# First quad's keys and queries by casting GpSimd transfers issued first, in place of float32 transfers and casts

## The chip, the cores and the metric

The kernel runs on one core of one Trainium2 chip. A time is the device time of one launch in microseconds (us); of several runs the median is given. "PE" is TensorE (the matrix engine), "DVE" VectorE, "ACT" ScalarE, "POOL" GpSimd, and "SP" SyncE. ACT, SP and POOL can each start transfers (DMAs); a transfer started from POOL may change the number type on its way (here float32 in memory to bf16 on the chip), one started from ACT or SP copies.

## The reference, cut to what matters

```
q_l, k_l, v_l: [8 batches, 8 heads, 512, 64]      q_g, k_g, v_g: [8, 8, 32, 64]      float32
out_g = softmax(q_g @ [k_g, k_l]^T / 8) @ [v_g, v_l]                 # 32 global rows see all 544 keys
s_ll  = q_l @ k_l^T / 8, kept where |i - j| <= 32, else -1e9          # 512 local rows see a band ...
out_l = softmax([q_l @ k_g^T / 8, s_ll]) @ [v_g, v_l]                 # ... and the 32 global keys
x = concat([out_g, out_l]) as [8*544 tokens, 512]
h = x @ w_in        # 512 x 2048
out = (h * sigmoid(1.702 h)) @ w_out                                  # 2048 x 512, float32 [4352, 512]
```

## The kernel before, in words

Attention and the two-layer network are one program. Heads are handled four at a time: a *quad* is four heads of one batch, so each batch has two quads (`u` = 0 and 1). Batch 0's quads are `a = Quad(0)` and `c = Quad(1)`; later batches use `Wide` quads. The program's order is written out by hand (`tc.manual_schedule()`): every engine runs its own instructions in the order of the text, and waits only for data.

For a quad, the keys `rk` and queries `rq` (bf16, 128 partitions = 4 heads x 32 rows) are turned by DVE's 32x32 transpose into `kT` (`Tk`, L311) and into the query tile `qt` (`Tq`, L315). `ext` (L325) copies the turned global queries `qgT` into rows of `qt` beside the local ones. `B` (L339) writes the band into the score banks as a product of an identity and a bias; `S` (L356) adds the scores, in two rounds of windows (`S(0)`, `S(1)`); `X` (L384, L387) is ACT's exponential out of the banks into `e`; `K`/`XK` (L375, L411) are the scores against the global keys; `U`, `ekU` (L438, L423) sum probabilities and values, `R` (L462 to L466) takes reciprocals, `XL` (L471) scales into `xL`, the network's input. `h_mm` (L615) and `o_mm` (L655) are the network's two products; they are started as soon as `xL` of a batch is there, and from then on PE always has network work beside the next quads.

How the start is loaded, before the change. SP's queue brings the global queries of the first two quads in float32 (`load_g32("q")`, 64 KB, L137), then the two halves of the first quad's queries in float32 (`q32`, L150), then the global keys (`load_g32("k")`). ACT's queue brings the two halves of its keys (`k32`, L149). The float32 halves lie in a tile `early`. When they land, ACT casts the first key half and both query halves (`cast_act`, L782), DVE casts the second key half (L791) and the global queries and keys (`cast_g32`, L140). POOL first sets constants: `warm0`, ones, `bd` (a block mask), the ones columns of the value tiles, the triangle `step` (`affine_select`, L169), and the mask of the later batches (`mask_rest`, L228 to L230); from 3.57 us on it starts casting transfers: queries and keys of the second quad (`load(0, (1,))`, L81 and L82), global values (`load_turned`, L122 and L123), and then, in `load_rest()`, the values of batch 0 (L249, four transfers), the first weight `w_in` in eight transfers (L259, with the six `make_mask` copies, L225, ahead of the last two), the second weight `w_out`, the inputs of batch 1, and so on. All of POOL's transfers stand in one queue, q0, and are served in order. While nothing has landed, PE multiplies zeros (`fill`, L183): 21 times at the start, and 8 times between `B` and the first `S`.

The order of the first stage, as written:

```python
    cast_act(rk, k32, 0); cast_act(rq, q32, 0); cast_act(rq, q32, 1); cast_g32("q", rqg)
    transpose_g(0, 2, "q"); a.ext((0, 1)); a.Tk(0, 8)
    nc.vector.tensor_copy(rk[:, 0, halves[1]], k32[:, halves[1]])
    a.Tk(8, 16); a.Tq(0, 8); a.Tq(8, 16); a.ext((2, 3)); cast_g32("k", rkg); transpose_g(0, 2, "k")
    load_rest(); a.B(0); a.B(1, split=True); fill(8, a.bk[1][3])
    a.S(0, added=True, part=0); a.S(0, added=True, part=1); a.X(0); a.S(1, ...); zero(2, ...); a.X(1)
    c.Tq(); c.ext(); c.Tk(); c.B(0); a.K(); a.XK(); c.B(1, ...); c.S(0, added=True); c.X(0)
```

`S(0)` is split in two parts: part 0 needs the first half of the queries, part 1 also the second half.

Of the kernel before, what the change touches and what calls it, by code (L numbers as in the profile page):

```python
# [20 lines left out]
def kernel(  # L21
# [110 lines left out]
    def load_g32(name, src):  # L132
        t = g32[name] = consts.tile([128, 2, D], F32, name="g32%s" % name)
        if name == "v":
            load_turned(nc.sync, t, src[:, 0:2, :])
        else:
            nc.sync.dma_start(out=t, in_=src[:, 0:2, :])  # L137

    def cast_g32(name, t):
        nc.vector.tensor_copy(t[:, 0:2, :D], g32[name])  # L140

    load(0, kq=False)
    rk, rq = loaded[0]
    early = ld.tile([128, 4, TB], F32, name="early", bufs=1)
    k32, q32 = (early[:, 2 * i : 2 * i + 2].rearrange("p a b -> p (a b)") for i in range(2))
    halves = (slice(0, 8 * D), slice(8 * D, 16 * D))
    load_g32("q", qgf)
    for f in halves:
        nc.scalar.dma_start(out=k32[:, f], in_=kf[0][:, 0, f])  # L149
        nc.sync.dma_start(out=q32[:, f], in_=qf[0][:, 0, f])  # L150
    load_g32("k", kgf)


    warm0 = consts.tile([128, 128], BF16)
    nc.gpsimd.memset(warm0, 0.0)
    step = consts.tile([128, 289], BF16)
    nc.vector.memset(step, 1.0)
    ones32 = consts.tile([128, 32], BF16)
    nc.gpsimd.memset(ones32, 1.0)
    nc.gpsimd.memset(rvg[:, :, D:], 1.0)  # L160
    bd = consts.tile([128, 4, 32], BF16)
# [4 lines left out]
    for i in range(2):  # L166
        vtiles.append(consts.tile([128, 8 * 5 * (D + 2)], BF16, name="v%d" % i))
        nc.gpsimd.memset(v_view(i, 4 + i)[:, :, :, :, D:], 1.0)
    nc.gpsimd.affine_select(  # L169
        out=step, in_=step, pattern=[[1, 289]], compare_op=ALU.is_ge,  # L170
        fill=0.0, base=-97, channel_multiplier=-1,
    )
    w_in_sb = wts.tile([128, 4, NKC, d_ff // 4], BF16)
# [4 lines left out]
    warm = consts.tile([128, 512], BF16)  # L178
    nc.vector.memset(warm, 0.0)

# [5 lines left out]

    qtiles = []
    for i in range(4):
        qt = consts.tile([128, 24, 32], F32, name="q%d" % i)
        nc.vector.memset(qt[:, 0:4, :], 0.0)  # L190
        nc.vector.memset(qt[:, 20:24, :], 0.0)
        qtiles.append(qt)

# [37 lines left out]

    mask_rest()
    load(0, (1,))
    load_turned(nc.gpsimd, rvg[:, 0:2, :D], vgf[:, 0:2])

    qgT = consts.tile([128, NQ, 40], F32)
    nc.vector.memset(qgT[:, :, 32:], 0.0)
    kgT = consts.tile([128, NQ, 32], F32)
    def transpose_g(lo, hi, names="qk"):
# [49 lines left out]
    class Quad:  # L289
# [31 lines left out]

        def ext(self, cs=(0, 1, 2, 3)):
            for c in cs:
                (r0, nr), t0, n = WIN[c], (0, 20, 1, 20)[c], (4, 3, 3, 4)[c]
                nc.vector.tensor_copy(  # L325
                    self.qt[:, t0 : t0 + n, r0 : r0 + nr],
                    qgT[:, self.Q, : n * nr].rearrange("p (t r) -> p t r", t=n))
# [293 lines left out]

    spot = consts.tile([128, 2], F32)
    nc.gpsimd.memset(spot, 0.0)

    spot_p = consts.tile([1, 2], BF16)
# [154 lines left out]

    def cast_act(r, f32, hf):
        nc.scalar.activation(r[:, 0, halves[hf]], f32[:, halves[hf]], AF.Copy)  # L782
# [23 lines left out]
    zero(2, a.bk[1][3])  # L806
    a.X(1)
    c.Tq()
    c.ext()
    c.Tk()  # L810
    c.B(0)
# [42 lines left out]
    gelu(gTs[0][:, 2:4, :], pt[1])  # L854
    c.G()
    for fc in range(4, FC):
        h_step(0, fc)
# [337 lines left out]
```

## Time and profile before

| | us |
|---|---|
| median of 3 runs (288.1 to 288.44) | 288.11 |
| the profiled execution | 287.94 |
| its span, first to last instruction | 286.0 |
| PE busy | 280.4 (98%) |
| DVE busy / ACT busy / POOL busy | 205.3 / 184.5 / 95.3 |
| share of the 16 DMA engines' span: q0 (POOL's transfers) / q1 (SP's) / q10 (ACT's) | 55.9% / 11.5% / 0.7% |

Times in the text are counted from the start of the span. A row of the timeline reads: start, duration, engine, line of the program, operation, tile written <- tiles read, how many, and in brackets how long the engine stood idle before it and what ended that. In the list of transfers the last number is the median time from issue to landing. "q" behind an engine's name marks its sequencer, which issues transfers.

### The profile page before, as it was taken

What the parts mean: (1) busy time and instruction counts of PE and PEld (TensorE: products, weight loads), DVE (VectorE), ACT (ScalarE), POOL (GpSimd) and SP (SyncE); (2) the same over time, 40 slices, a digit from 0 to 9 for tenths busy, and PEclk for the clock granted to TensorE, in tenths of its full rate; (3) what the DMA queues carried; (4) which work ended last, traced back from release to release, by engine and by line L of the source; (5) the groups of instructions that cost most, each with busy time, mean ns of one, the idle gap of its engine ahead of it and who ended that gap; (6) DMA issues with size and microseconds to landing.
All of it is one profiled execution on the core that took longest, in us unless ns stands there. A gap on an engine that the chain in (4) does not pass through costs nothing.

```text
span 286.0 us, 8845 instructions
## 1 busy us (share of the span) xinstructions
PE 280.4 (98%) x3727; PEld 179.5 (63%) x3727; DVE 205.3 (72%) x494; ACT 184.5 (65%) x297; POOL 95.3 (33%) x142
## 2 busy tenths in 40 slices
PE   8999999999999999999999999999999999999995
PEld 7544445544554488646884488647874589448884
DVE  7771367787689898679867998679867697363452
ACT  4847657568678784778649774877658761874331
POOL 8984550855946003920086004800040000000001
PEclk9999999999999999999999999999999999999999
DMA  7999995999999801993059803940122003200213
GB/s 203 156 191 207 203 165 79 147 224 130 155 175 187 151 3 48 94 191 60 10 88 150 147 2 77 100 66 5 28 51 73 2 3 76 73 0 2 73 35 115
DMA packets 59351, 28.23 MB, mean 99 GB/s; under 512 B 47472, under 2 KB 49776, under 8 KB 59312
## 3 DMA queue, kind: packets, MB, share of 16 engines
q0 software_dynamic: 51760, 17.83, 55.9%
q1 hardware_dynamic: 7120, 9.18, 11.5%
q8 instruction: 29, 0.48, 0.7%
q10 hardware_dynamic: 432, 0.66, 0.7%
q14 instruction: 10, 0.08, 0.1%
HBM read 36.31 MB, written 8.91 MB: 158 GB/s over the span
## 4 chain that ended last, share of the span: by engine, by line
PE 93%; DVE 2%; ACT 2%; DMA 1%; issue 0%; SPq 0%; DVEq 0%
PE hp L615 38%; PE px L726 13%; PE py L726 9%; PE op L655 9%; PE x L726 6%; PE s L560 6%; PE ov L586 5%; PE s L615 2%; DMA early<-in_q_l_dram 1%; DVE xL L471 1%; ACT e L384 1%; PE og L597 1%; PE s L356 1%; PE s L339 1%; ACT e L387 1%; DVE rs L466 1%
## 5 line engine op out<-in xcount | busy, mean ns | idle before, releaser
L615 PE MATMUL hp<-xL,w_in_sb 128*128 128x512 bf16 x480 | 105.4, 379 | 0.1
L615 PEld LDWEIGHTS <-w_in_sb 128*128 128x128 bf16 x576 | 56.1, 98 | 60.0 <-issue 0.4
L620 ACT ACTIVATE gT<-hp 128x512 bf16<-128x512 f32 x120 | 69.8, 597 | 23.9 <-PE hp L615 22.4
L571 ACT ACTIVATE e<-s 128x1016 bf16<-128x1016 f32 (+1 forms) x56 | 53.3, 1002 | 20.3 <-PE s L560 20.2
L726 PEld LDWEIGHTS <-gs 128*128 128x128 bf16 x480 | 46.2, 98 | 6.7
L699 DVE TENSOR_TENSOR gs<-gT 128x512 bf16<-128x512 bf16 (+1 forms) x90 | 30.3, 364 | 17.7 <-ACT gT L620 17.2
L576 POOL TENSOR_TENSOR e<-e,mask 128x1760 bf16<-128x1760 bf16 x4 | 13.3, 3320 | 81.1 <-ACT e L571 81.1
L98 POOL DMA_DIRECT2D v<-in_v_l_dram x40 | 31.0, 777 | 14.9 <-PE og L597 3.9
L726 PE MATMUL py<-wsum,gs 128*128 128x256 bf16 x240 | 30.3, 273 | 0.0
L655 PE MATMUL op<-w_out_sb,gT 128*128 128x512 bf16 x128 | 29.5, 380 | 0.0
L576 DVE TENSOR_TENSOR e<-e,mask 128x1712 bf16<-128x1712 bf16 (+1 forms) x24 | 25.2, 1049 | 5.6 <-ACT e L571 5.6
L512 DVE STREAM_TRANSPOSE kT<-rk 128x512 f32<-128x512 f32 x14 | 14.6, 1045 | 14.9 <-DMA rk<-in_k_l_dram 14.9
L759 POOL DMA_DIRECT2D out_dram<-ob x2 | 1.2, 598 | 69.7 <-ACT ob L113 69.5
L655 PEld LDWEIGHTS <-gT 128*128 128x128 bf16 x128 | 11.8, 98 | 13.9
L726 PEld LDWEIGHTS <-gT 128*128 128x128 bf16 x192 | 18.0, 98 | 2.7
L726 PE MATMUL px<-w_out_sb,gT 128*128 128x256 bf16 x160 | 19.2, 273 | 0.0
L726 PE MATMUL px<-w_out_sb,gs 128*128 128x256 bf16 x160 | 19.1, 273 | 0.0
L471 DVE TENSOR_TENSOR xL<-ov,rs 128x512 bf16<-128x512 f32 x27 | 17.8, 685 | 0.7 <-PE ov L438 0.2
L696 DVE TENSOR_TENSOR gs<-gT 128x1024 bf16<-128x1024 bf16 (+1 forms) x30 | 17.4, 579 | 0.0
L560 PEld LDWEIGHTS <-kT 32*128 32x128 bf16 x672 | 12.6, 93 | 7.6 <-issue 6.7
L113 ACT ACTIVATE ob<-px 128x512 f32<-128x512 f32 x10 | 6.0, 598 | 15.2 <-DVE zz L748 15.2
L560 PE MATMUL s<-q,kT 32*128 32x160 bf16 (+1 forms) x448 | 14.9, 246 | 0.0
(150 smaller groups left out, 360.3 us busy)
## 6 DMA issues: line engine op xcount, KB each, us to landing
out_dram<-ob SPq DMA_DIRECT2D x128, 64.0 KB, 3.0
rq<-in_q_l_dram POOLq DMA_DIRECT2D x5, 512.0 KB, 8.0
rk<-in_k_l_dram POOLq DMA_DIRECT2D x5, 512.0 KB, 10.0
v<-in_v_l_dram POOLq DMA_DIRECT2D x24, 96.0 KB, 4.9
w_in_sb<-in_moe_w_in_dram POOLq DMA_DIRECT2D x8, 256.0 KB, 8.3
w_out_sb<-in_moe_w_out_dram POOLq DMA_DIRECT2D x4, 512.0 KB, 10.3
rq<-in_q_l_dram POOLq DMA_DIRECT2D x5, 256.0 KB, 8.5
rk<-in_k_l_dram POOLq DMA_DIRECT2D x5, 256.0 KB, 7.9
```

The lines of the kernel that those rows point to most:

```text
L98: nc.gpsimd.dma_start(out=vt[0:n, hs, c, :D], in_=vs[FIRST[c] : FIRST[c] + n, hs])
L471: nc.vector.tensor_mul(self.x[:, 2 * self.u + h, :], self.st[1 + h], self.st["rs"])
L512: nc.vector.transpose(flat[:, 0:Sl].rearrange("p (r t) -> p t r", t=16), loaded[self.b][0][:, self.u].bitcast(F32))
L560: nc.tensor.matmul(bank(self.ps, j)[:, at : at + n], lhsT=self.k[p, KEYS[c] : KEYS[c] + 128, e], rhs=qs[p, :, :, e], start=(e == 0), stop= ...
L571: nc.scalar.activation(self.E[rnd][:, 2 * i : 2 * i + 2, :n], self.ps[i][:, :, :n], AF.Exp, scale=scale)
L576: eng.tensor_mul(e, e, mask[:, rnd : rnd + 1, :n].to_broadcast([128, 4, n]))
L615: nc.tensor.matmul(hp[:, : width(i)], lhsT=w_in_c[:, fc // 4, kc, fc % 4 // 2, :, fc % 2], rhs=(xL[i] if i < B else xG)[:, kc, :], start=( ...
L620: nc.scalar.activation(out_, in_, AF.Gelu_apprx_sigmoid)
L655: nc.tensor.matmul(op, lhsT=gTs[i][:, fc, tci * 128 : tci * 128 + 128], rhs=w_out_sb[:, fc, :], start=(first and fc == 4 * f4), stop=(fc = ...
L696: nc.vector.tensor_tensor(sums[i][2][:, g, :n], t[:, g, 0, :n], t[:, g, 1, :n], ALU.add)
L699: nc.vector.tensor_tensor(sums[i][k][:, g, : n // 2], x[:, g], y[:, g], op)
L726: nc.tensor.matmul(out_, lhsT=lv[:, g, tt * 128 : tt * 128 + 128], rhs=rv[:, g, :], start=(g == 0 and k in ((1, 3, 4, 6) if self.apart els ...
```

## The change

Local keys and queries of the first quad are no longer brought as float32 by the queues of ACT and SP and then cast; POOL's casting transfers bring them straight into `rk` and `rq`, in four halves. They are POOL's first instructions: both key halves, then the triangle (`affine_select`), then both query halves, then the global keys of two quads (`load_g(0, 2, "k")`), then the second quad's keys and queries (keys first; before, queries first), and only then POOL's other constants and the global values. The global queries still come as float32 by SP's queue; their cast, and the first two copies of `ext`, go from DVE to ACT. An `exp_table()` call stands ahead of them on ACT. `warm0` and `spot` are set by DVE instead of POOL; DVE clears the query tiles of quads 0 and 1 only, and those of 2 and 3 after `c.G()`; the zero tile `warm` is set after the global keys' transpose. `mask_rest` moves from ahead of POOL's transfers into `load_rest`, ahead of the `make_mask` copies. `fill(8)` becomes `fill(2)`. For the second quad, `Tk` and `ext` now come ahead of `Tq`.

```diff
     def load_g32(name, src):
         t = g32[name] = consts.tile([128, 2, D], F32, name="g32%s" % name)
-        if name == "v":
-            load_turned(nc.sync, t, src[:, 0:2, :])
-        else:
-            nc.sync.dma_start(out=t, in_=src[:, 0:2, :])
-
-    def cast_g32(name, t):
-        nc.vector.tensor_copy(t[:, 0:2, :D], g32[name])
+        nc.sync.dma_start(out=t, in_=src[:, 0:2, :])
...
     load_g32("q", qgf)
     for f in halves:
-        nc.scalar.dma_start(out=k32[:, f], in_=kf[0][:, 0, f])
-        nc.sync.dma_start(out=q32[:, f], in_=qf[0][:, 0, f])
-    load_g32("k", kgf)
+        nc.gpsimd.dma_start(out=rk[:, 0, f], in_=kf[0][:, 0, f])
     warm0 = consts.tile([128, 128], BF16)
-    nc.gpsimd.memset(warm0, 0.0)
+    nc.vector.memset(warm0, 0.0)
     step = consts.tile([128, 289], BF16)
     nc.vector.memset(step, 1.0)
+    spot = consts.tile([128, 2], F32)
+    nc.vector.memset(spot, 0.0)
+    nc.gpsimd.affine_select(out=step, ...)
+    for f in halves:
+        nc.gpsimd.dma_start(out=rq[:, 0, f], in_=qf[0][:, 0, f])
+    load_g(0, 2, "k")
+    nc.gpsimd.dma_start(out=rk[:, 1], in_=kf[0][:, 1])
+    nc.gpsimd.dma_start(out=rq[:, 1], in_=qf[0][:, 1])
     ones32 = consts.tile([128, 32], BF16)
     nc.gpsimd.memset(ones32, 1.0)
     nc.gpsimd.memset(rvg[:, :, D:], 1.0)
+    load_turned(nc.gpsimd, rvg[:, 0:2, :D], vgf[:, 0:2])
+    (value tiles' ones columns, then bd)
...
-    nc.vector.memset(warm, 0.0)
-    for i in range(4): (clear qtiles[i])
+    clear_q(0, 1)
...
-    mask_rest()
-    load(0, (1,))
-    load_turned(nc.gpsimd, rvg[:, 0:2, :D], vgf[:, 0:2])
...
             if part == 3:
+                mask_rest()
                 for m in MASKS:
                     make_mask(m)
...
-    cast_act(rk, k32, 0)
-    cast_act(rq, q32, 0)
-    cast_act(rq, q32, 1)
-    cast_g32("q", rqg)
+    exp_table()
+    on_act(rqg[:, 0:2, :D], g32["q"])
     transpose_g(0, 2, "q")
-    a.ext((0, 1))
+    a.ext((0, 1), on_act)
     a.Tk(0, 8)
-    nc.vector.tensor_copy(rk[:, 0, halves[1]], k32[:, halves[1]])
     a.Tk(8, 16)
     a.Tq(0, 8)
     a.Tq(8, 16)
     a.ext((2, 3))
-    cast_g32("k", rkg)
     transpose_g(0, 2, "k")
+    nc.vector.memset(warm, 0.0)
     load_rest()
     a.B(0)
     a.B(1, split=True)
-    fill(8, a.bk[1][3])
+    fill(2, a.bk[1][3])
...
     a.X(1)
+    c.Tk()
+    c.ext()
     c.Tq()
-    c.ext()
-    c.Tk()
     c.B(0)
...
     c.G()
+    clear_q(2, 3)
```

More of the change, by code (lines that the diff above doesn't have):

```diff
@@ L144 @@
     early = ld.tile([128, 4, TB], F32, name="early", bufs=1)
-    k32, q32 = (early[:, 2 * i : 2 * i + 2].rearrange("p a b -> p (a b)") for i in range(2))
     halves = (slice(0, 8 * D), slice(8 * D, 16 * D))
@@ L148 @@
     for f in halves:
-        nc.scalar.dma_start(out=k32[:, f], in_=kf[0][:, 0, f])
-        nc.sync.dma_start(out=q32[:, f], in_=qf[0][:, 0, f])
-    load_g32("k", kgf)
+        nc.gpsimd.dma_start(out=rk[:, 0, f], in_=kf[0][:, 0, f])
     warm0 = consts.tile([128, 128], BF16)
-    nc.gpsimd.memset(warm0, 0.0)
+    nc.vector.memset(warm0, 0.0)
     step = consts.tile([128, 289], BF16)
     nc.vector.memset(step, 1.0)
+    spot = consts.tile([128, 2], F32)
+    nc.vector.memset(spot, 0.0)
+    nc.gpsimd.affine_select(
+        out=step, in_=step, pattern=[[1, 289]], compare_op=ALU.is_ge,
+        fill=0.0, base=-97, channel_multiplier=-1,
+    )
+    for f in halves:
[3 more added lines that the diff above has]
+    nc.gpsimd.dma_start(out=rq[:, 1], in_=qf[0][:, 1])
     ones32 = consts.tile([128, 32], BF16)
@@ L160 @@
     nc.gpsimd.memset(rvg[:, :, D:], 1.0)
+    load_turned(nc.gpsimd, rvg[:, 0:2, :D], vgf[:, 0:2])
+    for i in range(2):
+        vtiles.append(consts.tile([128, 8 * 5 * (D + 2)], BF16, name="v%d" % i))
+        nc.gpsimd.memset(v_view(i, 4 + i)[:, :, :, :, D:], 1.0)
     bd = consts.tile([128, 4, 32], BF16)
@@ L165 @@
         nc.gpsimd.memset(bd[32 * r : 32 * r + 32, j, :], 1.0)
[L166 to L172, printed above, removed]
     w_in_sb = wts.tile([128, 4, NKC, d_ff // 4], BF16)
@@ L185, with clear_q @@
     fill(21, psP.tile([128, 512], F32, name="w", tag="p"), True)
[L187 to L192, printed above, removed]
+    qtiles = [consts.tile([128, 24, 32], F32, name="q%d" % i) for i in range(4)]
+    def clear_q(*quads):
+        for i in quads:
+            nc.vector.memset(qtiles[i][:, 0:4, :], 0.0)
+            nc.vector.memset(qtiles[i][:, 20:24, :], 0.0)
+    clear_q(0, 1)
+    qgT = consts.tile([128, NQ, 40], F32)
+    nc.vector.memset(qgT[:, :, 32:], 0.0)
+    kgT = consts.tile([128, NQ, 32], F32)
     WIN = ((0, 10), (6, 12), (14, 12), (22, 10))
@@ L230, in mask_rest @@
         nc.gpsimd.memset(mask_at(1, 236, 16, 12)[96:128, :, 8:12], 0.0)
-    mask_rest()
-    load(0, (1,))
-    load_turned(nc.gpsimd, rvg[:, 0:2, :D], vgf[:, 0:2])
-    qgT = consts.tile([128, NQ, 40], F32)
-    nc.vector.memset(qgT[:, :, 32:], 0.0)
-    kgT = consts.tile([128, NQ, 32], F32)
     def transpose_g(lo, hi, names="qk"):
@@ L320, in T, with ext @@
             self.Tq()
-        def ext(self, cs=(0, 1, 2, 3)):
+        def ext(self, cs=(0, 1, 2, 3), copy=nc.vector.tensor_copy):
             for c in cs:
                 (r0, nr), t0, n = WIN[c], (0, 20, 1, 20)[c], (4, 3, 3, 4)[c]
-                nc.vector.tensor_copy(
+                copy(
                     self.qt[:, t0 : t0 + n, r0 : r0 + nr],
@@ L620, in gelu @@
         nc.scalar.activation(out_, in_, AF.Gelu_apprx_sigmoid)
-    spot = consts.tile([128, 2], F32)
-    nc.gpsimd.memset(spot, 0.0)
     spot_p = consts.tile([1, 2], BF16)
@@ L779, in zero @@
             nc.tensor.matmul(ps, lhsT=warm[:, 0:128], rhs=warm, start=False, stop=False, skip_group_check=True)
-    def cast_act(r, f32, hf):
-        nc.scalar.activation(r[:, 0, halves[hf]], f32[:, halves[hf]], AF.Copy)
-    cast_act(rk, k32, 0)
-    cast_act(rq, q32, 0)
-    cast_act(rq, q32, 1)
-    cast_g32("q", rqg)
+    exp_table()
+    on_act(rqg[:, 0:2, :D], g32["q"])
     transpose_g(0, 2, "q")
-    a.ext((0, 1))
+    a.ext((0, 1), on_act)
     a.Tk(0, 8)
-    nc.vector.tensor_copy(rk[:, 0, halves[1]], k32[:, halves[1]])
     a.Tk(8, 16)
```

## The prediction

> **What bounds the kernel now.** I read the page's busy times first, then the chain that ended last over the first 18 us (start, length, what), then the timelines of the engines, then the transfers' times to landing.
>
> ```profile
> PE 280.4 (98%) x3727; PEld 179.5 (63%) x3727; DVE 205.3 (72%) x494; ACT 184.5 (65%) x297; POOL 95.3 (33%) x142
> ```
> PE is busy nearly throughout, so only what PE waits for, or does in vain, can be saved. Its 5.6 us of idle time and its zero products lie mostly in the first 18 us; this change touches nothing later except through its transfers.
>
> ```profile
> 0.81 0.46 SPq L137
> 1.28 0.06 issue
> 1.34 4.16 DMA early<-in_q_l_dram
> 5.50 0.02 issue
> 5.52 1.27 ACT rq L782 x2
> 6.79 0.02 issue
> 6.81 0.46 DVE q L315
> 7.27 0.04 issue
> 7.31 0.47 PE s L356 x16
> 7.78 1.65 ACT e L387 x2
> 9.43 0.04 issue
> 9.47 0.63 PE s L339 x6
> ```
> The reader sees the start hang on one thing: the first quad's queries land at 5.50, ACT casts two halves, DVE turns the second one, and part 1 of the first scores starts at 7.31. From there on PE and ACT hand over to each other without idle time up to 17.8 us, where the network's products begin. What is saved ahead of 7.31 is saved at the end, unless another wait takes its place.
>
> ```profile
> 10.01 1.05 DVE L311 STREAM_TRANSPOSE kT<-rk 128x512 f32<-128x512 f32 x1 [0.48 <-DMA rk<-in_k_l_dram]
> 11.12 0.66 PE L356 MATMUL s<-q,kT 32*128 32x200 bf16 x16
> 32.85 1.04 DVE L512 STREAM_TRANSPOSE kT<-rk 128x512 f32<-128x512 f32 x1 [10.20 <-DMA rk<-in_k_l_dram]
> 37.30 0.53 PE L560 MATMUL s<-q,kT 32*128 32x160 bf16 x16
> ```
> Two such waits stand close behind. The second quad's keys land just before 10.01, and its scores start at 11.12, 0.06 us after the turned keys: no slack. Batch 1's keys land at 32.83, at the end of the stream of weights; DVE's and ACT's preparation for its scores ends at 36.02, and PE comes to them at 37.30: 1.27 us of slack.
>
> **The change part by part.** The sum is made in the profiled execution (287.94: span 286.0 and 1.94 around it; the median is 0.17 above it).
>
> *Casts taken away.* ACT's three (0.63 each) and DVE's second key half (0.40) and global keys (0.61) go. Of these 1.27 us lie on the chain, between 5.52 and 6.79; the others lie beside it.
>
> *When POOL issues.* POOL's, ACT's and SP's first instructions start at 0.81. An issue costs 0.71 for POOL's first (L81) and 0.56 for the next (L82); the triangle takes 0.37 from its start to the next start. So key halves at 0.81 and 1.52, triangle at 2.08 (DVE set `step` by 1.25 before; one small clear more ahead of it), query halves at 2.45 and 3.01, global keys at 3.57 (0.71, as L128), second quad's keys at 4.28 and queries at 4.84, done at 5.40.
>
> *When they land.* No row has a 128 KB casting transfer first in the program. Bounds: from below ACT's 128 KB of packets took 2.88 us from issue; from above a 256 KB casting one took 4.32 from an idle queue, less 0.65 for half of it (w_in's 256 KB pieces land 1.3 us apart in the full stream) makes 3.67. I take 3.24, which a 96 KB casting one took at 115.5 us, the nearest in size, kind and idle queue:
>
> ```profile
> rq<-in_q_l_dram POOLq DMA_DIRECT2D x1, 256.0 KB, 4.3
> v<-in_v_l_dram POOLq DMA_DIRECT2D x1, 96.0 KB, 3.2
> ```
> Key halves then land at 4.05 and, 0.65 later, 4.70; the first query half at 2.45 + 3.24 = 5.69 (the keys ahead of it would allow 5.35), the second at 6.34. With the ends for 3.24, the second lands at 5.99 or 6.77.
>
> *What follows.* DVE turns keys at 4.05 to 4.70 and 4.70 to 5.32 (0.60, 0.62), queries at 5.69 to 6.14 and 6.34 to 6.79 (0.45 each), against 7.26 before: 0.47 us. ACT's cast of the global queries waits for 3.86 at the latest and takes about 0.3 (ACT's 128x128 copy at 35.5: 0.26); the transpose is done by 4.5, and two copies on ACT (0.26 each) by 5.0: hidden behind the query half at 5.69. Uncovered they would cost 0.5. PE does 16 band products to 5.80 and 2 fills to 6.05; six fills fewer, 0.64 us, cost nothing before and would have ended at 6.65, so taking them away is needed but is no gain of its own.
>
> *Second quad.* Behind the second query half come 32 KB of global keys (rvg's 24 KB landed 0.25 behind the keys: 6.6), then 256 KB twice. These landed 1.73 apart before, and 1.25 in the full stream (half of w_out's 2.5); with 1.5, keys at 8.1 and queries at 9.6. DVE: keys to 9.15, ext (0.60) to 9.75, queries (0.71) to 10.46. PE comes at 11.12 - 0.47 = 10.65: 0.19 of slack; with 1.73 it would be 10.5 landing, 10.9 to 11.2 turned, and the gain is gone. Keys first is worth the 0.34 between the two turns, behind the last landing.
>
> *The stream behind.* POOL comes to batch 0's values later: 5.40, two small sets, global values 0.81 and 0.55, value tiles' and bd's sets 0.29 and 0.80: 8.0 against 6.24. But before, the first value transfer landed 0.45 behind the global values, so the engines that move the data were the limit, not POOL. Their work is the same bytes (2.3 us saved at q1 and q10 come back in q0) begun some 0.5 later. I take 0.4 for the stream's delay; bounds 0 and 1.76. Deadlines, with 0.47 off PE's times: fourth value transfer landed 15.01, needed by c.U(1) at 16.65; fourth w_in 20.00, needed at 21.66; batch 1's keys as above. They leave 1.2, 1.2 and 0.8: 0.4 fits. mask_rest (1.06) ahead of the masks puts w_in's last two issues at about 19.0 instead of 16.09; the sixth landed at 22.33, so the engines still have work for 3 us: nothing. POOL also waits, before an issue, for the transfer eight before it (20.29 followed a landing at 20.00, 21.34 one at 21.05); in the new order these landings are long past.
>
> *The rest.* clear_q(2, 3), four times 0.17, moves to about 22 us, where DVE is idle until 32.8; `warm` (0.27) goes behind the keys' transpose near 7.2, ahead of zero products at 8.4. Nothing.
>
> Sum: -0.47, rounded to -0.45: 287.49 for the profiled execution, **287.66** for the median.
>
> **A rule against the change.** DVE's cast of the global keys took 0.61 at 7.33 while POOL issued, and 0.23 for the same form at 3.88 with POOL issuing too: a collision of 0.38, once in two. The Trainium skill, SBUF — State Buffer, section "SBUF: two separate sides", says that a DVE copy in a two-port mode locks GpSimd out of writing descriptors, and advises the hardware queues instead. By that rule what goes on POOL here could start late by as much as DVE's eligible operations beside it; the trace shows the collision from DVE's side only.
>
> **The rivals.**
> (1) *Landing as by the hardware queue.* With 2.88 the second query half lands at 5.99, gain 0.82; PE then stops at the second quad's queries or at batch 1's keys (1.27 - 0.4), about -0.75: 287.36. For it: POOL's data packets start some 0.8 behind the end of an issue. Against: no load of POOL's landed in under 2.7, and that one had 48 KB.
> (2) *Second quad takes the place of the first.* Its queries land at 10.4, as its keys did at 9.99 before with the hardware queues helping: gain 0 to 0.1: 288.1. The 1.73 speaks for it, 1.25 against.
> (3) *The weights' stream moves by POOL's delay* (slower). If it shifts by 1.76, batch 1's keys land at 34.6, its preparation ends at 37.8, PE stands 0.5 after 37.30: 288.6; each 0.1 more that POOL takes adds 0.1. It decides from a shift of 1.27, and is a loss of 0.2% from 1.85. Against it: 0.45 between the landings named above.
> (4) *VectorE holds POOL's issues* (slower). Identity, band and bias on DVE (2.60 to 3.45) follow the triangle, exactly where the queries are issued. If all 0.85, and the small clears ahead of them (0.3), are lost, the second query half lands at 7.5, turned at 7.95: 0.7 later, 288.8. It decides from a hold of 0.47. For it: the collision above. Against: POOL's issue at 4.27 took 0.56 beside DVE copies.
> (5) *PE stays slow.* Fills came 0.107 us apart up to 6.65, band products 0.16; after 9.47 six of these took 0.63. If PE, idle from 6.05 for a late query, keeps its slow pace to about 10, 1.7 us of products ahead of 11.12 take some 1.1 more: 288.8. The profile's granted clock is 1.00 throughout and can't tell. The Trainium skill, TensorE: Matmul & The Clock Gate, section "What's actually happening", has a gate that doubles the rate after a busy window of about 3.4 us; the fills' pace agrees, its threshold no run here shows.
>
> **How the numbers follow.** Forecast 0.42 (gain 0.1 to 0.8; some 0.19 of it beyond 0.2%), rival 1 0.22, rival 2 0.08, rival 3 0.14, rival 4 0.09, rival 5 0.05. A difference of 0.2%, 0.58 us, is about what a measurement can tell from none. Faster: 0.19 + 0.21 = 0.40. Slower: most of rivals 3 to 5, 0.25. Within: 0.35. The range goes from rival 1 with a little more, 287.2, to rivals 3 to 5 at 288.8, leaving out about 0.16. The forecast's own is 287.3 to 288.0.
>
> **What would show it.** Query half 2 landed at 6.0 to 6.8 and turned by 7.2; first scores' part 1 at about 6.85; second quad's queries turned by 10.5 and its scores at 10.65; first w_in product near 17.4 instead of 17.8; batch 1's keys at 33.2, with no PE gap ahead of its scores. Wrong if POOL's issues take over 0.8 in the first 5 us, if a query lands past 6.8, if the scores' products stay 0.1 apart after 7, or if PE stands near 16, 21 or 37 us.

## The result, and the profile after

| | before | after |
|---|---|---|
| median, us | 288.11 (288.1 to 288.44) | **290.89** (290.4 to 293.05) |
| ratio to before | | 1.0104, 95% interval 1.0078 to 1.0131 |
| profiled execution / its span | 287.94 / 286.0 | 293.05 / 291.0 |
| first quad: last key half / last query half landed | 4.95 / 6.12 (float32) | 5.35 / 7.79 (bf16) |
| first exponentials (`X(0)`) start | 7.76 | 8.77 |
| second quad's last transfer landed | 9.99 | 13.30 |
| second quad's scores start on PE | 11.12 | 14.09 |
| first network product starts | 17.82 | 21.68 |
| batch 1's keys landed / its scores start | 32.83 / 37.30 | 38.84 / 42.05 |

The change costs 2.8 us, 1.0% (by the interval 2.2 to 3.8 us); the forecast was 287.66, range 287.2 to 288.8. The profiled execution of after is the longest of its four; the other three took 290.4, 290.4 and 291.38, so its times show where the loss arises and overstate how large it is at the median.

Busy times and granted clock in the page of after:

```profile
PE 281.1 (97%) x3721; PEld 179.4 (62%) x3721; DVE 203.5 (70%) x491; ACT 183.6 (63%) x298; POOL 97.8 (34%) x145
PEclk9979999999999999999999999999999999999999
```

PE's busy time hardly moved (280.4 before), so the loss is idle time, and work at a lower clock: the third slice (14.6 to 21.8 us) has a granted clock of 0.7 of full speed, where before every slice had the full one.

The chain that ended last, in after (start, length, what):

```profile
0.71 0.63 issue
1.34 1.25 POOL rk L142 x2
...
3.14 1.02 POOL rq L155 x2
...
8.30 0.78 POOL v L244
9.08 8.43 DMA v<-in_v_l_dram
...
17.79 0.71 POOL w_in_sb L255
...
19.68 2.30 POOL mask L227 x6
...
25.26 13.58 DMA rk<-in_k_l_dram
...
38.86 1.05 DVE kT L508
...
42.05 0.65 PE s L556 x24
```

Before, the chain left the transfers at 5.50 and then ran through ACT and PE. Here it runs through POOL and its queue for 39 us: first POOL's issues one behind the other, then the values, for which POOL waits before its sixth weight transfer, then the masks, then batch 1's keys.

The start of after on the engines (start, length, engine, line; in brackets the idle time before and what ended it):

```profile
1.34 1.25 POOL L142 DMA_DIRECT2D rk<-in_k_l_dram  x2 [0.82 <-POOLq L1167]
...
3.04 1.12 POOL L155 DMA_DIRECT2D rq<-in_q_l_dram  x2
...
4.81 0.60 POOL L157 DMA_DIRECT2D rk<-in_k_l_dram  x1
...
7.82 0.45 DVE L311 STREAM_TRANSPOSE q<-rq 128x256 f32<-128x256 f32 x1 [0.50 <-DMA rq<-in_q_l_dram]
8.32 0.92 PE L352 MATMUL s<-q,kT 32*128 32x80 bf16 x32 [0.43 <-DVE q L311]
11.62 1.04 DVE L307 STREAM_TRANSPOSE kT<-rk 128x512 f32<-128x512 f32 x1 [2.76 <-DMA rk<-in_k_l_dram]
11.88 0.71 POOL L255 DMA_DIRECT2D w_in_sb<-in_moe_w_in_dram  x1 [0.34 <-DMA rk<-in_k_l_dram]
13.32 0.71 DVE L311 STREAM_TRANSPOSE q<-rq 128x512 f32<-128x512 f32 x1 [0.41 <-DMA rq<-in_q_l_dram]
13.58 2.10 POOL L255 DMA_DIRECT2D w_in_sb<-in_moe_w_in_dram  x3 [0.99 <-DMA rq<-in_q_l_dram]
14.09 0.72 PE L352 MATMUL s<-q,kT 32*128 32x200 bf16 x16 [1.94 <-DVE q L311]
16.76 0.70 POOL L255 DMA_DIRECT2D w_in_sb<-in_moe_w_in_dram  x1 [1.07 <-DMA v<-in_v_l_dram]
```

Three things are to be read here. POOL's first transfer starts at 1.34, not 0.81, and the second query half can be turned only at 7.82. PE then stands 1.94 us for the second quad's queries, which land at 13.30. And POOL itself stands three times (0.34, 0.99, 1.07) ahead of a weight transfer, each time until the transfer eight before it has landed: one late landing holds up what is issued behind it.

The trace also has the landing of each transfer on each of the 16 DMA engines. For the second quad's two transfers (us; "lag" is last minus median engine):

```
                        issued        median engine    15th          last            lag
before (queries, keys)  3.57  4.27     7.36   8.91      8.10   9.86    8.26   9.99   0.90  1.08
after  (keys, queries)  4.81  5.37     8.81  10.42     11.27  12.74   11.60  13.30   2.79  2.88
```

Thirteen of the 16 engines have the keys by 9.40; the last two have them at 11.27 and 11.60, and the lag is still there for the values behind them (the first: 15th engine 13.64, last 16.47). These times are of one execution of each kernel, so they show where a transfer was late; how late it is in another execution can differ.

### The profile page after: what moved, and what is told of

The parts are those of the page before. It is cut to its first block, busy times and chain, and to the rows that moved or that the text cites. A ratio compares the mean times of both kernels' runs of the same rounds, so it can differ in the third digit from the quotient of the medians.

```text
span 291.0 us, 8828 instructions
## 1 busy us (share of the span) xinstructions
PE 281.1 (97%) x3721; PEld 179.4 (62%) x3721; DVE 203.5 (70%) x491; ACT 183.6 (63%) x298; POOL 97.8 (34%) x145
## 4 chain that ended last, share of the span: by engine, by line
PE 82%; DMA 8%; POOL 5%; DVE 3%; issue 1%; ACT 0%; POOLq 0%; DVEq 0%
PE hp L611 34%; PE px L719 13%; PE py L719 9%; PE op L648 7%; PE x L719 6%; PE s L556 6%; PE ov L582 5%; DMA rk<-in_k_l_dram 5%; DMA v<-in_v_l_dram 3%; PE s L611 1%; POOL mask L227 1%; POOL w_in_sb L255 1%; DVE xL L467 1%; PE og L593 1%; DVE rs L462 0%
## 5 line engine op out<-in xcount | busy, mean ns | idle before, releaser
L508 DVE STREAM_TRANSPOSE kT<-rk 128x512 f32<-128x512 f32 x14 | 14.6, 1041 | 16.7 <-DMA rk<-in_k_l_dram 16.7
## 6 DMA issues: line engine op xcount, KB each, us to landing
w_out_sb<-in_moe_w_out_dram POOLq DMA_DIRECT2D x4, 512.0 KB, 10.4
```

What stands on the lines that cost most here:

```text
L508: nc.vector.transpose(flat[:, 0:Sl].rearrange("p (r t) -> p t r", t=16), loaded[self.b][0][:, self.u].bitcast(F32))
```

## The experiments

All ratios are to executions of the kernel before that were taken beside the run (their medians lie between 288.05 and 288.56), with 95% intervals; so they are not the quotients of the medians in the table. The ratio of e5 leaves out its longest execution, 294.01.

| run | median, us | ratio | 95% interval |
|---|---|---|---|
| e11 before, without the second quad's transfers | 287.73 | 0.9987 | 0.9978 to 0.9995 |
| e7 before, second quad's keys first | 288.11 | 1.0003 | 0.9994 to 1.0011 |
| e6 before, 2 fills instead of 8 | 288.21 | 1.0002 | 0.9991 to 1.0013 |
| e13 changed, queries by hardware queues, second quad issued later | 288.45 | 1.0002 | 0.9987 to 1.0016 |
| e4 changed, queries by hardware queues | 288.63 | 1.0020 | 1.0009 to 1.0030 |
| e10 changed, without the second quad's transfers | 289.10 | 1.0044 | 1.0028 to 1.0059 |
| e2 changed, first quad by hardware queues and casts | 289.36 | 1.0039 | 1.0022 to 1.0057 |
| e12 changed, second quad issued 1.15 us later | 289.95 | 1.0065 | 1.0052 to 1.0077 |
| e14 changed, first quad in whole transfers | 290.01 | 1.0058 | 1.0037 to 1.0080 |
| e1 before, first quad by POOL alone | 290.17 | 1.0068 | 1.0056 to 1.0080 |
| e5 changed, more fills | 290.87 | 1.0085 | 1.0061 to 1.0109 |
| the change | 290.89 | 1.0104 | 1.0078 to 1.0131 |
| e9 changed, `bd` ahead of the first transfer | 291.12 | (one execution) | |
| e8 changed, second quad by hardware queues | 291.68 | 1.0115 | 1.0098 to 1.0132 |
| e3 changed, zero products ahead of the second quad | 291.85 | 1.0124 | 1.0111 to 1.0138 |

### Which part of the change costs? (e1, e2, e6, e7)

e1 is the kernel before with the first quad brought by POOL; of the rest of the change it has only `warm0` set by DVE:

```diff
     for f in halves:
-        nc.scalar.dma_start(out=k32[:, f], in_=kf[0][:, 0, f])
-        nc.sync.dma_start(out=q32[:, f], in_=qf[0][:, 0, f])
+        nc.gpsimd.dma_start(out=rk[:, 0, f], in_=kf[0][:, 0, f])
     ... (step, then its affine_select, moved up to here)
+    for f in halves:
+        nc.gpsimd.dma_start(out=rq[:, 0, f], in_=qf[0][:, 0, f])
...
-    cast_act(rk, k32, 0); cast_act(rq, q32, 0); cast_act(rq, q32, 1)
-    nc.vector.tensor_copy(rk[:, 0, halves[1]], k32[:, halves[1]])
```

> The kernel before with only the load path changed: the first quad's keys and queries come by casting GpSimd transfers issued first (the triangle between keys and queries), ACT's and DVE's casts of them are gone; everything else, mask_rest, the order of the second quad, 8 fills, stays as before. Theory Q (one GpSimd queue now brings first and second quad behind each other, so both land late): about as slow as the changed kernel, 290 to 291.5. Rival M (the moved GpSimd work in load_rest and the late constants delay the weights): about as before, 288.1 to 288.6. Rival C (the lost fills and the wait cost PE its full rate): in between, 289 to 290, since the 8 fills are still there.

e2 is the changed kernel with the first quad again in float32 by the queues of ACT and SP, and with the casts; DVE again casts the global queries and does the first two copies of `ext`:

```diff
-        nc.gpsimd.dma_start(out=rk[:, 0, f], in_=kf[0][:, 0, f])
+        nc.scalar.dma_start(out=k32[:, f], in_=kf[0][:, 0, f])
+        nc.sync.dma_start(out=q32[:, f], in_=qf[0][:, 0, f])
...
-    for f in halves:
-        nc.gpsimd.dma_start(out=rq[:, 0, f], in_=qf[0][:, 0, f])
...
+    cast_act(rk, k32, 0); cast_act(rq, q32, 0); cast_act(rq, q32, 1)
... (cast of the global queries, ext and the second key half on DVE, as before)
```

> The changed kernel with only the load path undone: the first quad's keys and queries come as float32 by the queues of ACT and SP, with the casts of before; the global keys, the second quad, mask_rest, 2 fills and the late clears stay as changed. Theory Q: as before or a little faster, 287.5 to 288.3, with the second quad's transfers issued 2 us earlier. Rival M: slow as the changed kernel, 290 to 291. Rival C: 288.5 to 289.5, since 6 fills are still missing.

e6 and e7 are the kernel before with `fill(2)` for `fill(8)`, and with the second quad's keys ahead of its queries:

```diff
-    fill(8, a.bk[1][3])
+    fill(2, a.bk[1][3])
```
```diff
-    load(0, (1,))
+    nc.gpsimd.dma_start(out=rk[:, 1], in_=kf[0][:, 1])
+    nc.gpsimd.dma_start(out=rq[:, 1], in_=qf[0][:, 1])
...
-    c.Tq(); c.ext(); c.Tk()
+    c.Tk(); c.ext(); c.Tq()
```

> The kernel before with 2 fills instead of 8. Theory G: PE idles 0.6 us before the first scores, and in some executions a half-rate stretch of 3.4 us follows: 288.5 to 289.3, with more spread. Theory Q alone: as before, 288.1 to 288.4.

> The kernel before with only the second quad's order changed: its keys issued and turned ahead of its queries. Theory Q: last landing stays, the turn behind it is 0.34 shorter, but PE comes to the second quad's scores at the same time: no difference, 287.9 to 288.4. A rival that has the order cost something: 288.6 and more.

Fills and order are worth nothing (1.0002 and 1.0003). The loads alone cost 2.0 us. The timeline of e1:

```profile
7.54 0.45 DVE L315 STREAM_TRANSPOSE q<-rq 128x256 f32<-128x256 f32 x1 [0.16 <-DMA rq<-in_q_l_dram]
9.82 0.71 DVE L315 STREAM_TRANSPOSE q<-rq 128x512 f32<-128x512 f32 x1 [1.27 <-DMA rq<-in_q_l_dram]
11.40 1.04 DVE L311 STREAM_TRANSPOSE kT<-rk 128x512 f32<-128x512 f32 x1 [0.28 <-DMA rk<-in_k_l_dram]
12.51 0.66 PE L356 MATMUL s<-q,kT 32*128 32x200 bf16 x16 [0.64 <-DVE eg L397]
```

The first quad is turned 0.73 us later than before, though its casts are gone. The second quad, issued only at 6.30 and 6.82 because the first quad's and the constants stand ahead of it on POOL, lands at 9.80 and 11.38, and its scores start 1.39 later.

e2, at 289.36, missed the range of Theory Q (287.5 to 288.3) and lies in that of rival C (288.5 to 289.5), so the change's rearrangement is no remedy by itself. There POOL is free of the first quad and issues the second quad's transfers at 2.63 and 3.19, while the hardware queues (those of ACT and SP) still bring the first; both run over the same 16 engines, and the first quad's second query half lands at 7.11 instead of 6.12. The first exponentials start at 8.75, 0.99 later than before. The second quad lands early (8.65 and 10.00) and gains nothing by it, for its scores start only 2.2 us after its queries are turned:

```profile
10.03 0.71 DVE L311 STREAM_TRANSPOSE q<-rq 128x512 f32<-128x512 f32 x1
12.97 0.67 PE L352 MATMUL s<-q,kT 32*128 32x200 bf16 x16
```
```profile
9.30:12.80 3.50, 3.17 (x28) 1.71 (x22) 1.67 (x7) 3.07 (x7) 3.45 (x6) 0.51 2.29 161
```

The last row is a stretch of time: PE was busy for 3.17 of these 3.50 us, at a granted clock of 0.51 of full speed. That is rival C's mechanism, PE losing its full rate; it is taken up below.

### How much is the first quad, how much the second? (e10, e11)

Both kernels without the second quad's two transfers; that quad's keys and queries are then taken from the first quad's tiles, so part of the input is not read:

```diff
-    nc.gpsimd.dma_start(out=rk[:, 1], in_=kf[0][:, 1])
-    nc.gpsimd.dma_start(out=rq[:, 1], in_=qf[0][:, 1])
...
-    loaded[self.b][0][:, self.u]
+    loaded[self.b][0][:, 0 if self.Q == 1 else self.u]
```

> The changed kernel without the second quad's keys and queries: their two transfers are left out, and the second quad works on the first quad's. Theory Q: its wait is gone; against the kernel before with the same left out, only the first quad's lateness of 0.9 to 1.1 us remains, so about 288.6 to 289.3 here. If the first quad's lateness were hidden, 288.0; if the rest of the change cost as much, 290 and more.

> The kernel before without the second quad's keys and queries: their two transfers are left out, and the second quad works on the first quad's. Theory Q: the second quad was not late, PE gets to it no sooner: 287.6 to 288.2.

Without the second quad's transfers the changed kernel is at 289.10 and the kernel before at 287.73: 1.4 us remain, which the second quad cannot have caused. These transfers themselves cost 1.8 us in the changed kernel (290.89 - 289.10) and 0.4 before (288.11 - 287.73). So, by the medians, the loss of 2.8 divides evenly: 1.4 from the first quad and from the stream begun later, 1.4 from the second quad's lateness and what follows it. With the interval of the whole loss, 2.2 to 3.8, the second part is known only to lie between 0.9 and 2.4. In the trace of e10, the first quad's exponentials start at 8.65, 0.9 later than before, and the first network product at 18.66, 0.84 later:

```profile
8.65 1.66 ACT L381 ACTIVATE e<-s 128x856 bf16<-128x856 f32 x2 [4.15 <-PE s L350]
18.66 3.63 PE L609 MATMUL s<-xL,w_in_sb 128*128 128x512 bf16 x16
```

### Why does the first quad come late? (e4, e9, e14)

e9 sets `bd` on POOL ahead of the first key transfer instead of near the end of its constants, as a test of whether the 0.63 us of "issue" ahead of it is a fixed price:

```diff
+    bd = consts.tile([128, 4, 32], BF16)
+    nc.gpsimd.memset(bd, 0.0)
+    for j in range(4): ... nc.gpsimd.memset(bd[32 * r : 32 * r + 32, j, :], 1.0)
     for f in halves:
         nc.gpsimd.dma_start(out=rk[:, 0, f], in_=kf[0][:, 0, f])
```

> The changed kernel with the five small sets of bd (0.8 us of GpSimd work from 0.81 on) moved ahead of its first key transfer. In the changed kernel that transfer is shown from 1.34, not from 0.81 as forecast. If the 0.53 us are a preparation that runs beside other GpSimd work, the transfer starts at about 1.65 and the first key half lands near 5.0; if they are spent in the queue of GpSimd itself, it starts at 2.1 and lands near 5.5.

The chain of e9 at its start:

```profile
0.71 0.10 issue
0.82 0.21 POOL bd L142
...
1.56 0.11 POOL bd L145
1.67 0.34 POOL rk L147
```

POOL sets from 0.82 on, and the first transfer starts at 1.62 in the timeline (the chain counts it from 1.67), only 0.28 later than without the sets ahead of it, which take 0.85. So 0.57 of the 0.85 us of sets cost the transfer nothing: something that it needs ahead of its start runs beside other POOL work. Where the transfer comes first, this shows as 0.53 us lost (1.34 against 0.81).

e4 takes the changed kernel and brings the queries by the queues of ACT and SP in float32, with ACT's two casts:

```diff
-    for f in halves:
+    for f, eng in zip(halves, (nc.scalar, nc.sync)):
         nc.gpsimd.dma_start(out=rk[:, 0, f], in_=kf[0][:, 0, f])
+        eng.dma_start(out=q32[:, f], in_=qf[0][:, 0, f])
...
-    for f in halves:
-        nc.gpsimd.dma_start(out=rq[:, 0, f], in_=qf[0][:, 0, f])
...
+    for f in halves:
+        on_act(rq[:, 0, f], q32[:, f])
```

> The changed kernel with only the queries of the first quad as float32, one half by ACT's queue and one by SP's, cast on ACT; its keys stay GpSimd's first transfers. Theory Q: queries land near 4.5 and are cast by 5.5, the second quad's transfers move up by two 128 KB pieces (1.3 us): 287.6 to 288.8, within 0.3% of before. Rival M: 290 to 291. Rival C: 288.5 to 289.5.

With three queues at work the queries land at 3.87 and 4.65 and the keys at 5.58 and 6.22. The first quad is then complete 1.6 us earlier than in the changed kernel, casts and all, and the time falls to 288.63. What the float32 route pays in casts it gets back by its queues' earlier start (0.82) and by running over three queues at once; the runs do not tell the two apart. The rates of all transfers in 40 slices of the first 18 us, in the kernel before and then in the changed one, fit this (a casting transfer counts with the bytes that it writes):

```profile
GB/s 0 0 0 0 86 295 309 352 410 373 273 368 241 183 182 173 168 182 165 158 173 140 133 140 149 144 153 158 149 145 162 193 203 196 209 203 198 209 200 244
```
```profile
GB/s 0 0 0 0 97 48 30 141 184 184 93 105 141 186 145 108 150 146 187 168 173 115 135 148 153 134 153 141 184 141 151 139 135 142 132 141 132 123 150 144
```

From 1.8 to 6.3 us (the fifth slice to the fourteenth) the mean is 289 GB/s before and 121 after. The casting transfers have only half as many bytes of the first quad to write, but at 121 the half takes longer than the whole did at 289; even doubled, for the float32 that is read, the rate is 242.

e14 brings the first quad in whole transfers of 256 KB instead of halves:

```diff
-    for f in halves:
-        nc.gpsimd.dma_start(out=rk[:, 0, f], in_=kf[0][:, 0, f])
+    nc.gpsimd.dma_start(out=rk[:, 0], in_=kf[0][:, 0])
...
-    for f in halves:
-        nc.gpsimd.dma_start(out=rq[:, 0, f], in_=qf[0][:, 0, f])
+    nc.gpsimd.dma_start(out=rq[:, 0], in_=qf[0][:, 0])
```

> The changed kernel with the first quad's keys in one 256 KB transfer and its queries in one, instead of two halves each: the same bytes in three waiting transfers ahead of the second quad's instead of five, and these issued 1.1 us earlier, near 3.7 and 4.2. If the lag of single engines comes of the number of waiting transfers, it falls to 0.3 to 0.5 us (last engine against the median one) and the second quad lands near 9.0 and 10.4; the first quad's keys, whole, land near 5.4 and its queries near 7.3, so the time falls to some 290.0. If it comes of bytes still waiting, or of how early the issue stands, the lag stays at 2 us or more, the second quad lands at 11 to 13, and the time is 290.9 or more.

The timeline of e14:

```profile
2.51 0.59 POOL L153 DMA_DIRECT2D rq<-in_q_l_dram  x1
6.74 0.77 DVE L309 STREAM_TRANSPOSE q<-rq 128x256 f32<-128x256 f32 x2 [0.24 <-DMA rq<-in_q_l_dram]
7.25 1.51 PE L350 MATMUL s<-q,kT 32*128 32x120 bf16 x48 [1.90 <-DVE q L309]
10.40 0.71 DVE L309 STREAM_TRANSPOSE q<-rq 128x512 f32<-128x512 f32 x1
12.02 0.66 PE L350 MATMUL s<-q,kT 32*128 32x200 bf16 x16
```

Whole queries landed at 6.72, before even the first half (6.85) in the changed kernel; they were issued 0.53 earlier, with one issue of POOL less ahead of them. The time fell to 290.01, as expected for the case that the number of waiting transfers counts (about 290.0), and the second quad landed at 8.95 and 10.38 as that case has it (9.0 and 10.4), though its lag only fell to 0.9 and 1.0. A part of what is left of the loss is no landing: the second quad's queries are turned by 11.11, but its scores start at 12.02, for PE ran at half rate from 7.75 to 11.17, behind the 1.90 us of idle time in the third row.

### Why does the second quad come late? (e8, e12, e13, and e14 again)

e8 brings the second quad by the queues of ACT and SP in float32:

```diff
-    nc.gpsimd.dma_start(out=rk[:, 1], in_=kf[0][:, 1])
-    nc.gpsimd.dma_start(out=rq[:, 1], in_=qf[0][:, 1])
+    nc.scalar.dma_start(out=k32, in_=kf[0][:, 1])
+    nc.sync.dma_start(out=q32, in_=qf[0][:, 1])
...
+    on_act(rk[:, 1], k32)
+    on_act(rq[:, 1], q32)
```

> The changed kernel with the second quad's keys and queries as float32 by ACT's and SP's queues, cast on ACT; the first quad stays on GpSimd's queue. Theory Q: the second quad lands by 8 and no longer waits, the first quad's lateness of about 1 us stays: 288.9 to 289.6. If instead the second quad's landing were no cost of its own: 290.3 to 291.

At 291.68 this missed, and by the mechanism that e2 shows from the other side. In e8:

```profile
7.02 1.25 DVE L308 STREAM_TRANSPOSE kT<-rk 128x256 f32<-128x256 f32 x2 [1.16 <-DMA rk<-in_k_l_dram]
8.80 1.93 PE L353 MATMUL s<-q,kT 32*128 32x120 bf16 x48 [3.12 <-DVE q L312]
```

The second quad, which is wanted later, landed at 5.05 and 6.46, and POOL's four halves came behind it, at 6.99, 7.63, 8.28 and 8.95. ACT and SP issued at 0.82 and 1.33, POOL's first started at 1.34: what was issued first took the engines.

e12 changes only when the second quad's transfers, and the global values behind them, are issued: POOL's constants come ahead of them.

```diff
     load_g(0, 2, "k")
-    nc.gpsimd.dma_start(out=rk[:, 1], in_=kf[0][:, 1])
-    nc.gpsimd.dma_start(out=rq[:, 1], in_=qf[0][:, 1])
     ones32 ...; rvg's, the value tiles' and bd's sets
+    nc.gpsimd.dma_start(out=rk[:, 1], in_=kf[0][:, 1])
+    nc.gpsimd.dma_start(out=rq[:, 1], in_=qf[0][:, 1])
     load_turned(nc.gpsimd, rvg[:, 0:2, :D], vgf[:, 0:2])
```

> The changed kernel with GpSimd's constants (ones, the value tiles' columns, bd, about 1.3 us) set between the global keys' transfer and the second quad's, so that these are issued at about 6.1 instead of 4.81. Theory Q in its plain form (one queue, served in order, no idle engines): the second quad lands at the same time or up to 0.5 later: 290.5 to 291.3. Rival W (transfers issued while several others wait in the queue leave one or two of the 16 engines far behind, as 2.8 us here against 0.5 where they were issued at 6.3 in the kernel with the loads alone): the last landing comes earlier, near 11.5 instead of 13.3: 289.6 to 290.3.

e13 does the same to e4 (the diffs of e4 and e12 together).

> The changed kernel with the first quad's queries by the hardware queues and ACT casts, and with GpSimd's constants between the global keys and the second quad's transfers, so that these are issued some 1.7 us later than with the queries by hardware queues alone (near 5.5 and 6.0 instead of 3.77 and 4.31). If the lag of single engines comes of issuing into a full row of waiting transfers, the second quad lands near 9.3 and 10.7 instead of 9.58 and 11.17, its scores start near 11.5 instead of 11.96, and the time is 288.0 to 288.4, at or just under the kernel before. If the lag has nothing to do with the time of issue, the second quad lands 1.5 us later than there, near 11 and 12.7, and the time is 289.5 or more.

The timelines of e12 and of e13:

```profile
5.96 0.56 POOL L168 DMA_DIRECT2D rk<-in_k_l_dram  x1
9.80 1.05 DVE L307 STREAM_TRANSPOSE kT<-rk 128x512 f32<-128x512 f32 x1 [1.29 <-DMA rk<-in_k_l_dram]
11.20 0.71 DVE L311 STREAM_TRANSPOSE q<-rq 128x512 f32<-128x512 f32 x1
11.96 0.67 PE L352 MATMUL s<-q,kT 32*128 32x200 bf16 x16 [0.16 <-DVE q L311]
```
```profile
4.89 0.55 POOL L168 DMA_DIRECT2D rk<-in_k_l_dram  x1
8.73 1.05 DVE L307 STREAM_TRANSPOSE kT<-rk 128x512 f32<-128x512 f32 x1 [0.78 <-DMA rk<-in_k_l_dram]
10.23 0.71 DVE L311 STREAM_TRANSPOSE q<-rq 128x512 f32<-128x512 f32 x1
11.18 0.67 PE L352 MATMUL s<-q,kT 32*128 32x200 bf16 x16
```

And the landings of the second quad's transfers (first-issued, second-issued) on the 16 engines:

```
                                     issued         last            lag (last - median engine)
after                                4.81  5.37     11.60  13.30    2.79  2.88
e5, the same loads                   4.81  5.37     11.67  13.47    2.25  2.74
e3, the same loads                   4.83  5.39     10.82  12.28    1.76  1.40
e9, nearly the same                  5.09  5.65     11.19  12.51    1.39  0.97
e12 issued behind the constants      5.96  6.51      9.78  11.17    0.37  0.43
e14 the first quad whole             3.78  4.33      8.95  10.38    0.88  1.04
e4  queries by hardware queues       3.77  4.31      9.58  11.17    1.95  1.73
e13 the same, behind the constants   4.89  5.43      8.71  10.21    0.27  0.35
```

Twice, issuing the transfers over 1.1 us later made them land earlier: by 1.8 and 2.1 us in e12 against the changed kernel, and by 0.9 and 1.0 in e13 against e4. In e12 that is worth 0.94 us of the median (intervals 1.0052 to 1.0077 against 1.0078 to 1.0131). So early issue is no gain in itself, and what delays the second quad is not the bytes ahead of it, which are the same. It is not the hour of the issue either: e14 issues earliest of the kernels that load the first quad by POOL alone, and lags 0.9 to 1.0. The runs with a lag over 1.1 had at least four transfers unfinished when the first of the two was issued (after: one key half, two query halves, the global keys), e12, e13 and e14 three. That is no rule yet: the kernel before, e2 and e7 had six, most of them of the hardware queues, and the first of the two lagged 0.9, 0.6 and 0.3.

The trace's packets show a part of where the time went. The second quad comes in 256 packets of 2 KB, with a median of 0.17 us. In every kernel with a lag over 1.1 some of the 2 KB packets took over 1 us from 7 us on (in after two, 1.32 from 8.58 and 1.33 from 9.04; in e5 seven, up to 1.74; one or two in e3, e4 and e9), and in e12, e13 and e14 none did. (The kernel before and e2 had one and three, near 5.6, and little lag.) Why they took so long is not settled.

Further back e12 has a lag too, where nothing on the path waits: its last global values landed on the 15th engine at 11.54 and on the last at 13.02. That one may have another cause: a packet of 16 KB in the queue of instructions (q8) took 0.95 us from 10.85. In e1 and e13 as well the transfer in flight, or the next one, has its last engine over 1 us behind the 15th behind such a packet (10.88 and 10.13); which engine carried it the trace does not tell.

The Trainium skill, DMA: Bandwidth & Descriptors, section "Latency and other measured facts", says that two of the sixteen engines are usually the slower ones for transfers issued by GpSimd, and guesses that fetching their descriptors contends for a port. The two late engines of the changed kernel agree with that; the records here do not say which two they are.

e13 at 1.0002 is the best of the versions that load by POOL early; it stands level with the kernel before and does not beat it.

### Is it PE's clock? (e3, e5)

After the wait for the second quad PE ran at half rate in the profiled execution of after (stretch, then PE, weight loads, DVE, ACT, POOL, granted clock):

```profile
12.00:14.50 2.50, 0.56 (x19) 0.43 (x16) 1.74 (x7) 0.63 (x2) 1.51 (x3) 1.00 2.05 150
14.50:18.00 3.50, 3.50 (x60) 1.53 (x52) 1.68 (x3) 2.05 (x3) 2.10 (x4) 0.51 1.27 138
```

e5 asks whether the six fills taken away let PE go idle, and adds more of them around the first scores; e3 keeps PE busy with zero products while it waits for the second quad.

```diff
-    fill(2, a.bk[1][3])
+    fill(10, a.bk[1][3])
     a.S(0, added=True, part=0)
+    fill(4, a.bk[1][3])
     a.S(0, added=True, part=1)
```
```diff
+    zero(8, c.bk[1][1])
     c.S(0, added=True)
```

> The changed kernel with PE kept busy while it waits for the first quad's queries: 10 fills instead of 2 ahead of the first scores and 4 between their two parts (128 columns each). Theory G (the two idle gaps of about 1 us put PE at half rate for a 3.4 us stretch later, as the profiles of the changed kernel, of the one with its loads undone and of the one with 8 zero products show): the half-rate stretch is gone and 0.4 to 1.0 us come back, 289.9 to 290.5. Theory Q alone (the landings are all): no difference, 290.5 to 291.3.

> The changed kernel with 8 zero products of 512 columns on PE between the second quad's band products and its first scores (1.7 us where PE stood idle 2.2 us in the profiled execution). Theory Q: the wait stays, only the slow window behind it goes: 290.0 to 290.7, 0.2 to 0.8 less than changed. Rival C: most of the loss goes, 288.5 to 289. Rival M: no difference.

e5 shortened the gaps near 7 and 8 us, and its median is that of the change (290.87). Its profiled execution was the longest of its six (294.01), so only this is read from it: the half rate is there again, at 13.93 to 17.34, behind the wait for the second quad.

```profile
12.00:14.00 2.00, 0.19 (x3) 0.09 (x1) 1.49 (x6) 0.67 (x2) 0.91 (x2) 0.98 3.28 148
14.00:17.30 3.30, 3.04 (x48) 1.65 (x51) 1.11 (x4) 1.66 (x2) 2.48 (x4) 0.50 1.85 159
```

So in these two it follows that wait, not the missing fills. e3 missed all of its ranges (291.85) and does not settle it: its queries landed at 12.28 and the zero products ran from 12.89 to 14.82, behind the landing and so on the path, and half rate was at 9.55 to 12.96, behind an earlier gap. In e2 and e14, too, it came behind idle time ahead of and between the first scores (1.01 and 0.80 us; 1.90 us), and both have 2 fills. e6, the kernel before with 2 fills, had none (no execution had a mean clock below 0.997); e2 and e14 with more fills were not run, so there the fills remain a possible remedy.

When it comes can be read from the clock's changes, which lie 3.41 us apart or multiples of it. In the steps of 3.41 us that ended at a change to half rate PE was busy for 1.2 to 2.0 us (after 1.48, e5 1.67, e2 1.60, e14 1.51, e3 1.98, e8 1.23); steps at full rate with 2.2 us or more, in the first 20 us of all the traces (e10 2.21, e12 2.40, after 2.57 in the step ahead of that wait) were followed by full rate. (A step of e8 that was itself at half rate, with 2.35, was followed by another such.) The steps begin at another time in every execution, so how a gap falls into the steps differs from one execution to the next.

What the half rate costs depends on where it falls. From the second quad's scores to the first network product it is 7.59 us in after and 7.61 in e5, whose stretch lies there, and 6.70 to 6.93 in every other profiled execution: 0.7 to 0.9 us. In e2 the stretch lies ahead of the second quad's scores: from the first exponentials to these it is 4.22, against 3.36 before, again 0.9. Over whole executions it is less clear. In e12 three executions with a mean clock of 0.994 (one such stretch) have a median of 290.01 and three with 0.998 one of 289.89; in e14 the one at 1.000 was the slowest, 291.05; the kernel before ran 289.81 and 289.22 at 0.994 against a median of 288.56. The mean does not say where the stretch lay. So of the 3.9 us that the profiled execution of after has lost at the first network product, 0.7 to 0.9 is half rate, brought about by the wait for the second quad; what it is worth at the median stays open.

## Why the prediction was wrong, point by point

- **"When POOL issues", first transfer at 0.81: wrong by 0.53.** It was taken from the first instructions of ACT and SP. No transfer in the trace of before was POOL's first instruction; the first one there stood behind 2.8 us of other work. e9 shows that this time hides behind such work. The other issues came as forecast (0.69, 0.56, 0.58, 0.57), so rival 4, VectorE holding POOL's issues, is refuted for this place.
- **"When they land": the 3.24 from issue to landing was right for the first transfer alone.** Its lower bound, 2.88, was put down to 128 KB; that transfer was a key half in float32, 256 KB. The first key half took 3.36; the query halves took 3.81 and 4.20, against 3.24 and 3.33. Of the second half's error of 1.45 us (7.79 against 6.34), 0.58 is the later issue and 0.87 the longer landing. The turn ended at 8.27 against 7.26 before: the gain of 0.47 was a loss of 1.0. This is the first failed step, and e10 and e11 price it, with the stream begun later, at 1.4 us.
- **"Second quad", 9.6: wrong by 3.7, the largest single error.** This is the second failed step. The sum spaced the two transfers by a steady rate; but a transfer counts only when the last of its 16 engines has it. The query half ahead of it, 1.45 late, and a lag 1.8 longer than the 1.08 of before make 3.25 of it. Rival 2 had this place and gave it 0 gain, at a landing of 10.4; it had no row for so large a lag, since in the trace of before it was 0.9 to 1.1. (The case with 1.73 is also added up wrongly: 6.6 and twice 1.73 is 10.06, not 10.5.) Against the change, e10 and e11 price this at 1.4 us, half-rate stretch included, and e12 gets 0.9 of that back.
- **"The stream behind", 0.4 with an upper bound of 1.76: the first weight landed 4.1 us later** (19.79 against 15.66) and batch 1's keys 6.0 (38.84 against 32.83). The rule that POOL waits for the transfer eight before was seen in the trace of before and dismissed ("long past"); with the second quad late it cost POOL 0.34, 0.99 and 1.07, and more behind the values. Rival 3 had the stream moved, with a cause too small.
- **Rival 5, PE's slow pace, happened, and for nearly the 1.1 us it was given (0.7 to 0.9).** In the changed kernel it came behind the wait for the second quad and not for want of fills (e5). In e2 and e14 it stood where the rival had its loss, ahead of the second quad's scores; in e9 PE kept its slow pace from the start for longer (eight band products took 1.38 at 10.22, where six took 0.63 before; the clock's first change is at 11.72).
- **Right:** the six fills (e6) and the order of the second quad (e7) are worth nothing by themselves; ACT's cast and copies for the global queries stayed hidden (done by 4.5, the query half came at 6.85). `mask_rest` behind the stream can be told from e2, where its last weights were issued later than before, the seventh at 17.32, and still landed earlier (23.76 against 24.45). In the changed kernel itself its 1.2 us (18.49 to 19.68) stand on the chain that ended last, so there it is not shown to cost nothing.

The chance of 0.25 for slower was too low, and in the main for one reason: each row for a landing was of a transfer with an idle queue or a full steady stream, and the change made something that the trace did not have, seven transfers in one queue within 5 us from an empty start, of which the last two were on the path.

## What to carry to other kernels

A transfer that casts on its way saves the cast, but if it moves work from three queues into one it can cost more than the cast did, as here; add up when the last piece of everything in that queue is needed, not only the first. Count a transfer as landed when the last of the DMA engines has it, look at the lag between engines in the trace, and try issuing the not-so-urgent ones later, or in fewer pieces, before issuing them earlier. If a wait leaves PE idle, look for a half-rate stretch behind it and price that with the wait. Where an engine's first instruction becomes a transfer, don't price its start by another engine's.

## What the runs showed of the hardware that was not expected

- A transfer issued 1.15 us later landed 1.8 us earlier (e12 against after), where one or two of 16 engines otherwise finished up to 2.9 us behind the median one (1.4 to 2.8 for the first of the two in e9, e3, e5 and after, whose loads are the same or nearly so).
- Two halves of 128 KB completed later than one whole of 256 KB: 7.79 against 6.72 for the queries (e14), which were issued 0.53 earlier.
- POOL's first transfer started 0.53 us later than the first of ACT and SP, and that time can be covered: 0.85 us of sets ahead of it moved it by 0.28 (e9).
- PE's clock halved for 3.41 us behind steps of 3.41 us in which PE was busy for 2.0 us or less, and not behind steps at full rate with 2.2 or more; on the path one such stretch cost 0.7 to 0.9 us.
- Transfers of POOL and of the hardware queues delayed each other by about 1 us where they ran together: the first quad's queries by 0.99 in e2 (7.11 against 6.12), by 1.16 in e8 (8.95 against 7.79).
